# The first block of a fused convolution and MLP kernel: other load order, first weight unit rounded in thirds, copies on another queue, output weights combined later

## Chip, cores and metric

One core of one Trainium2 chip runs the whole kernel. The metric is device time in microseconds (us), the median of several executions. A profiled span is about 1.7 us shorter than the time the same execution reports (2428.01 beside 2429.71 for the kernel before), so spans are compared with spans and times with times.

## The reference

A causal depthwise convolution with 7 taps, softmaxed per head, then `silu(x @ w_in) @ w_out`, over 32768 tokens of 192 channels with 2048 hidden columns:

```python
w = np.exp(weight - weight.max(-1, keepdims=True))        # (8 heads, 7 taps)
w = w / (w.sum(-1, keepdims=True) + 1e-9)
x_pad = zeros(pad) ++ x                                   # pad = 6 positions in front of each sequence
out = einsum('hk,bskhg->bshg', w, windows(x_pad))         # (8, 4096, 192) -> 32768 x 192
h = out @ w_in                                            # w_in arrives as float64
g = h * (1 / (1 + exp(-h)))
return (g @ w_out).astype(float32)
```

(Shortened; `zeros`, `++` and `windows` stand for the padding and indexing code.)

## The kernel before

The tokens go through in 32 blocks of 1024. Blocks 2 to 32 use a recombined product scheme, laid out in a plan of slots. The first block is plain: while it is transposed, convolved and multiplied, the weights are loaded in four units of `w_in` and four of `w_out`. They are 64-bit words, which VectorE takes apart and rounds to float32 with integer operations (`rounded`). `ws` is a copy of a rounded unit `wr` with the two partition halves swapped. GpSimd combines some of the weights for the later scheme. The parts that matter here:

```python
def load(b):                                   # x of a block: 12 DMAs, three channel thirds k of four
    nat = nats[b] = xpool.tile(...)
    for k in range(NK):
        for i in range(P // SQ):
            (nc.sync if b or k or i % 2 else nc.scalar).dma_start(out=nat[...], in_=x_v[...])

# ... wexp (taps) on nc.scalar, six values of x on nc.gpsimd ...
load(0)

def rounded(dst, key, shared):                 # whole unit: 768 columns per instruction
    # eight VectorE operations + two on ScalarE (shared) or two more on VectorE
    # ...

def round_in(j):
    rounded(wr[j].rearrange("p a k c -> p (a k c)"), ("i", j), j < 2)
    for e in range(2):
        nc.scalar.dma_start(out=ws[j][R * e : R * e + R], in_=wr[j][R - R * e : 2 * R - R * e])

load_in(0, nc.scalar)
load_in(1, nc.sync)
# ... softmax of the taps: max, subtract, Exp on ScalarE, sum, reciprocal, ...

for k in range(NK):                            # first block
    turn_in(0, k)                              # transpose
    for i in range(K):
        conv(0, k, i)                          # seven taps on VectorE
    spread(0, k)                               # four DMAs nat -> dup
    if k == 0:
        round_in(0)
        load_in(2, nc.sync)
round_in(1)
load_in(3, nc.sync)
for j in range(NJ):
    up_plain(0, j)                             # 64x512 matmuls into 8 PSUM banks, Silu on ScalarE
    # ... round_in(j + 2) or round_out, load_out, load(1) ...
# ... conv of block 2, combine_in, plain down-projection ...
for j in range(NJ):
    combine_out(j)
```

`raw`, the tile that a unit is loaded into, comes from a pool of three buffers (`tag="t"`) that also serves `two`, the scratch of the rounding. `nat` and `dup` have one buffer each.

## Time and profile before

| | kernel before |
|---|---|
| time, median | 2429.41 us (3 runs, 2428.07 to 2429.82) |
| profiled span | 2428.0 us |
| TensorE busy | 98% |
| VectorE busy from first transpose to the second unit | 9.77 to 39.85 us without a gap |
| TensorE ends k=2 of the first up-projection | 40.46 us |
| TensorE runs without a gap from | 43.12 us |
| block 2, first product | 117.81 us |
| TensorE's end, to the end of the span | 2417.55, 10.47 us |

To read it: from 43.12 us on TensorE is the chain until close to the end, so the total is a start, a body of fixed length and a tail. The prediction shows the lines that carry this.

The executions of the kernel before in all the rounds below fall into two groups, at 2427.9 to 2428.4 and at 2429.1 to 2430.9. The profile above is of the longer group (2429.71).

### The profile page before, as it was taken

How to read it: one execution, taken by the hardware profiler on the slowest of the kernel's cores; microseconds unless marked ns; L12 is line 12 of the kernel's file. 1: busy time of each engine (PE TensorE's matmuls, PEld its weight loads, DVE VectorE, ACT ScalarE, POOL GpSimd, SP SyncE). 2: the span in 40 equal slices, each digit the busy share in tenths (PEclk: the TensorE clock that was granted, in tenths of full speed). 3: DMA queues.
4: the chain of work that ended last, by engine and by line, in shares of the span. 5: the costliest groups of instructions: out<-in, count | busy, mean ns of one | idle time of the engine just before them, and what ended most of it. 6: DMA issues, size and time to landing. Idle time of an engine off the chain costs nothing.

```text
span 2428.0 us, 42997 instructions
## 1 busy us (share of the span) xinstructions
PE 2391.3 (98%) x17744; PEld 939.2 (39%) x17744; DVE 2075.0 (85%) x2810; ACT 980.8 (40%) x1840; POOL 62.0 (3%) x92
## 2 busy tenths in 40 slices
PE   5999999999999999999999999999999999999998
PEld 3334433344333344333443333443334433334432
DVE  8898888898888988888988889888889888898875
ACT  2145433345333454333453334543334533345432
POOL 2300000000000000000000000000000000000000
PEclk9999999999999999999999999999999999999999
DMA  7321222212222222222122222122221222222210
GB/s 153 75 44 35 36 53 53 40 38 38 45 53 43 42 39 36 53 53 40 38 38 44 53 44 46 35 36 53 53 40 38 37 45 53 43 43 39 36 40 14
DMA packets 452260, 111.64 MB, mean 46 GB/s; under 512 B 421792, under 2 KB 426912, under 8 KB 452064
## 3 DMA queue, kind: packets, MB, share of 16 engines
q1 hardware_dynamic: 447056, 105.84, 22.6%
q10 hardware_dynamic: 4784, 2.78, 0.6%
q8 instruction: 139, 2.28, 0.4%
q14 instruction: 57, 0.47, 0.1%
q0 software_dynamic: 224, 0.27, 0.0%
HBM read 31.49 MB, written 25.17 MB: 23 GB/s over the span
## 4 chain that ended last, share of the span: by engine, by line
PE 98%; DVE 1%; DMA 1%; ACT 0%; issue 0%; ACTq 0%; POOL 0%; SPq 0%; POOLq 0%; DVEq 0%
PE ps L411 48%; PE ps L468 46%; PE ps L519 2%; PE ps L375 1%; DMA nat<-in_x_dram 0%; DVE nat L325 0%; DVE two L111 0%; DMA raw<-in_moe_w_in_dram 0%; DVE cmb L570 0%; DVE mh L111 0%; DVE xt L305 0%; POOL out_dram L587 0%; SPq L165 0%; ACT L385 0%; DVE osb L580 0%
## 5 line engine op out<-in xcount | busy, mean ns | idle before, releaser
L411 PE MATMUL ps<-dup,ws 64*128 64x512 f32 x2480 | 869.9, 589 | 0.0
L468 PE MATMUL ps<-g,wo 128*32 128x512 f32 x2976 | 662.0, 593 | 0.0
L435 DVE TENSOR_TENSOR g<-u,ps 128x512 f32<-128x512 f32 x744 | 485.8, 680 | 119.1 <-PE ps L411 89.8
L411 PE MATMUL ps<-win,wr 64*128 64x512 f32 x1488 | 567.7, 589 | 0.0
L468 PE MATMUL ps<-t,wo 128*32 128x512 f32 (+1 forms) x4464 | 500.7, 450 | 0.0
L432 ACT ACTIVATE g<-g 128x512 f32<-128x512 f32 x744 | 444.7, 631 | 97.4 <-DVE g L435 97.4
L411 PEld LDWEIGHTS ps<-dup,ws 64*128 64x128 f32 x2480 | 363.0, 187 | 292.0 <-issue 277.9
L468 PE MATMUL ps<-t,wx 128*32 128x512 f32 x2976 | 453.1, 592 | 0.0
L325 DVE SCALAR_TENSOR_TENSOR nat<-xt,taps,nat 128x512 f32<-128x512 f32 x576 | 432.2, 750 | 15.1
L411 PE MATMUL ps<-dup,wr 64*128 64x512 f32 x992 | 419.9, 596 | 0.0
L426 ACT COPY u<-ps 128x512 f32<-128x512 f32 x496 | 277.7, 588 | 229.1 <-PE ps L411 226.1
L558 ACT COPY cmb<-ps 96x512 f32<-96x512 f32 x31 | 18.0, 581 | 832.1 <-PE ps L468 832.1
L452 DVE TENSOR_TENSOR t<-g 128x1024 f32<-128x1024 f32 x248 | 299.8, 1220 | 27.0 <-PE ps L468 27.0
L452 DVE TENSOR_TENSOR t<-g,t 128x1024 f32<-128x1024 f32 x248 | 303.4, 1224 | 17.9 <-PE ps L468 7.4
L411 PEld LDWEIGHTS ps<-win,wr 64*128 64x128 f32 x1488 | 233.4, 187 | 175.5 <-issue 147.2
L468 PEld LDWEIGHTS ps<-t,wo 128*32 128x32 f32 x4464 | 178.3, 110 | 222.6 <-issue 204.9
L411 PE MATMUL ps<-win,ws 64*128 64x512 f32 x496 | 242.2, 589 | 0.0
L468 PE MATMUL ps<-g,wx 128*32 128x512 f32 x1488 | 234.7, 592 | 0.0
L468 PEld LDWEIGHTS ps<-t,wx 128*32 128x32 f32 x2976 | 121.9, 110 | 278.2 <-issue 268.7
L570 DVE TENSOR_TENSOR cmb<-cmb,ps 96x512 f32<-96x512 f32 x155 | 105.7, 682 | 141.9 <-ACT u L555 139.7
L411 PEld LDWEIGHTS ps<-dup,wr 64*128 64x128 f32 x992 | 160.5, 187 | 128.2 <-issue 114.3
L468 PEld LDWEIGHTS ps<-g,wo 128*32 128x32 f32 x2976 | 168.5, 110 | 97.7 <-issue 97.7
(53 smaller groups left out, 1191.3 us busy)
## 6 DMA issues: line engine op xcount, KB each, us to landing
dup<-nat SPq DMA_DIRECT2D x384, 128.0 KB, 2.3
nat<-in_x_dram SPq DMA_DIRECT2D x382, 64.0 KB, 2.4
out_dram<-osb SPq DMA_DIRECT2D x376, 64.0 KB, 1.9
raw<-in_moe_w_out_dram SPq DMA_DIRECT2D x8, 384.0 KB, 3.5
raw<-in_moe_w_in_dram SPq DMA_DIRECT2D x12, 192.0 KB, 4.2
ws<-wr ACTq DMA_DIRECT2D x8, 192.0 KB, 5.6
raw<-in_moe_w_in_dram ACTq DMA_DIRECT2D x4, 192.0 KB, 5.9
xt<-xt SPq DMA_DIRECT2D x31, 4.5 KB, 1.9
```

The costliest lines, as they stand in the source:

```text
L325: nc.vector.scalar_tensor_tensor(out=dst, in0=src, scalar=tap, in1=dst, op0=ALU.mult, op1=ALU.add)
L375: nc.tensor.matmul(hs[a, n, e], rows(wr[j], e)[:, a, k, :], rows(d, e)[:, n, k, :], start=k == 0, stop=k == NK - 1,)
L411: nc.tensor.matmul(bk[b, m, bn], rows(w, half), rows(v, half), start=first, stop=True, skip_group_check=True,)
L426: pin(copy(u, bk[b, m, "1"]))
L432: pin(nc.scalar.activation(g, g, AF.Silu))
L435: pin(nc.vector.tensor_tensor(g, us.pop((b, m, i)), bk[b, m, bn], op=ALU.add))
L452: pin(nc.vector.tensor_tensor(t[i // 2][:, i % 2, :], u, v, op=ALU.subtract))
L468: nc.tensor.matmul(accs[b][i][SQ * q : SQ * q + SQ, cols], lhs[:, e, SQ * c : SQ * c + SQ], rhs[:, e, cols] if i < 5 else rhs[:, e, ts(q, ...
L519: nc.tensor.matmul(acc[k][R * n : R * n + R, :], wo[j][:, a, e, R * k : R * k + R], gs[b, j, a][:, n, e, :], start=j == 0 and a == 0 and e ...
L558: pin(nc.scalar.copy(c[0], acc[0][0:n, :]))
L570: pin(nc.vector.tensor_tensor(out_, u, v, op=ALU.add))
```

## The change

The intent is to have TensorE's long run begin sooner. The Exp table is loaded by a dummy before it is wanted, and four slow DMA issues leave ScalarE. The first unit of `w_in` is rounded a third at a time so that each third of channels can be multiplied as soon as it is convolved. The copies `ws` leave ScalarE's queue. The combination of `w_out` moves into the second block.

```diff
-    def load(b):
+    def load(b, ks=range(NK)):
...
-    load(0)
+    load(0, (0,))
+
+    warm = const.tile([P, 1], F32, name="warm")
+    vec.memset(warm, 0.0)
+    nc.scalar.activation(warm, warm, AF.Exp)
...
-    def round_in(j):
-        rounded(wr[j].rearrange("p a k c -> p (a k c)"), ("i", j), j < 2)
-
-        for e in range(2):
-            nc.scalar.dma_start(
+    def round_in(j, k=None):
+        ...
+        else:
+            rounded(wr[j][:, :, k, :], words[:, :, k], j < 2)
+        if k in (None, NK - 1):
+            del raws["i", j]
+            for e in range(2):
+                nc.gpsimd.dma_start(
                     out=ws[j][R * e : R * e + R], in_=wr[j][R - R * e : 2 * R - R * e]
                 )
...
-    load_in(0, nc.scalar)
+    load_in(0, nc.sync)
+    load(0, (1, 2))
     load_in(1, nc.sync)
...
         spread(0, k)
-        if k == 0:
-            round_in(0)
-            load_in(2, nc.sync)
+        round_in(0, k)
+    load_in(2, nc.sync)
     round_in(1)
...
-    for j in range(NJ):
-        combine_out(j)
...
-        run(b, plan[:NU])
+        run(b, plan[: NU // 4])
+        if b == 1:
+            for j in range(NJ):
+                combine_out(j)
+        run(b, plan[NU // 4 : NU])
```

More of the change, by code (lines that the diff above doesn't have):

```diff
@@ L118 @@
     nats, xts, gs = {}, {}, {}
-    def load(b):
-        nat = nats[b] = xpool.tile([P, NK, TB // SQ, SQ], F32, tag="nat", name="nat")
-        for k in range(NK):
+    def load(b, ks=range(NK)):
+        if b not in nats:
+            nats[b] = xpool.tile([P, NK, TB // SQ, SQ], F32, tag="nat", name="nat")
+        nat = nats[b]
+        for k in ks:
             for i in range(P // SQ):
@@ L172, in load_out, with rounded, like @@
             queue.dma_start(out=raw[:, a, :, :], in_=out32[a, q])
-    def rounded(dst, key, shared):
-        words = raws.pop(key).rearrange("p (n t) -> p n t", t=2)
-        lo, hi = words[:, :, 0], words[:, :, 1]
+    def rounded(dst, words, shared):
+        lo, hi = words[:, :, :, 0], words[:, :, :, 1]
+        x_, y_ = dst.shape[1:]
+        def like(t):
+            return t.rearrange("p (x y) -> p x y", x=x_)
+        n = x_ * y_
         two = tpool.tile([P, 4 * TB], I32, tag="t", name="two")
-        ex, st = two[:, 0:WC], two[:, WC : 2 * WC]
-        mh = xpool.tile([P, 4 * TB], I32, tag="cmb", name="mh")[:, 0:WC]
+        ex, st = like(two[:, 0:n]), like(two[:, n : 2 * n])
+        mh = like(xpool.tile([P, 4 * TB], I32, tag="cmb", name="mh")[:, 0:n])
         one = 1 << 20
@@ L213, in rounded @@
         )
-    def round_in(j):
-        rounded(wr[j].rearrange("p a k c -> p (a k c)"), ("i", j), j < 2)
-        for e in range(2):
-            nc.scalar.dma_start(
-                out=ws[j][R * e : R * e + R], in_=wr[j][R - R * e : 2 * R - R * e]
-            )
-    def round_out(q):
-        rounded(wo[q].rearrange("p a e d -> p (a e d)"), ("o", q), False)
+    def round_in(j, k=None):
+        words = raws["i", j].rearrange("p (a k c t) -> p a k c t", a=2, k=NK, t=2)
+        if k is None:
+            rounded(
+                wr[j].rearrange("p a k c -> p a (k c)"),
+                words.rearrange("p a k c t -> p a (k c) t"),
+                j < 2,
+            )
+        else:
[4 more added lines that the diff above has]
+                nc.gpsimd.dma_start(
+                    out=ws[j][R * e : R * e + R], in_=wr[j][R - R * e : 2 * R - R * e]
+                )
+    def round_out(q):
+        rounded(
+            wo[q].rearrange("p a e d -> p a (e d)"),
+            raws.pop(("o", q)).rearrange("p (a x t) -> p a x t", a=2, t=2),
+            False,
+        )
     def comb(out, u, v, op):
```

## The prediction

> **What bounds the kernel now.** I read the page first, then the chain of waits in order of time, then the timeline of the first 125 us engine by engine. Page, part 1 (engine, busy us, share, instructions):
>
> ```profile
> PE 2391.3 (98%) x17744; PEld 939.2 (39%) x17744; DVE 2075.0 (85%) x2810; ACT 980.8 (40%) x1840; POOL 62.0 (3%) x92
> ```
>
> TensorE (PE) is busy 98% of the 2428.0 us span. The chain (start, us, what) shows where it isn't:
>
> ```profile
> 39.88 0.47 ACTq L219
> 40.35 0.04 issue
> 40.39 0.75 ACTq L219
> 41.14 0.03 issue
> 41.17 1.28 ACT L385
> 42.45 0.01 issue
> 42.47 0.60 ACT g L385
> 43.07 0.04 issue
> 43.12 33.35 PE ps L375 x143
> 76.46 41.35 PE ps L519 x192
> 117.81 37.97 PE ps L411 x176
> 155.78 36.22 PE ps L468 x384
> ```
>
> From 43.12 on the chain is TensorE alone up to 2413.72; then 14.3 us of tail that the diff doesn't touch. So the time is (moment from which TensorE runs without a gap) + about 2370 + tail, and a change confined to the first block can move only that moment, and the clock TensorE has just after it. Blocks 2 to 32 repeat every 74.2 us (117.81, 192.00, ...) whatever the start was.
>
> What sets 43.12 is a serial line through VectorE (DVE) and then ScalarE (ACT). From the timeline (start, us, engine, line, op, count, idle before):
>
> ```profile
> 6.33 1.28 ACT L280 ACT_TABLE_LOAD   x1 [6.33 <-DMA nat<-in_x_dram]
> 8.60 0.22 DVE L111 TENSOR_TENSOR wexp<-wexp,wred 128x56 f32<-128x56 f32 x1
> 9.77 0.70 DVE L305 STREAM_TRANSPOSE xt<-nat 128x512 f32<-128x512 f32 x1
> 33.37 1.02 DVE L111 TENSOR_SCALAR two<-raw 128x768 int32<-128x768 int32 x2
> 35.81 4.65 PE L375 MATMUL ps<-dup,wr 64*128 64x512 f32 x16 [0.33 <-DMA dup<-nat]
> 38.89 0.96 DVE L111 SCALAR_TENSOR_TENSOR wr<-mh,two 128x768 f32<-128x768 f32 x1
> ```
>
> VectorE has no gap over 0.1 us from 9.77 to 39.85: third k=0 (transpose and 7 taps, to 15.6), the whole first w_in unit (15.64 to 21.39), k=1 (21.30), k=2 (27.17), the second unit (33.37 to 39.85). ScalarE then still has to issue two copies of ws (in its queue behind that unit), load the table for Silu and evict one bank: 3.26 us. TensorE was through at 40.46, and waits 2.66 us with full PSUM banks. That wait has a second price, in the windows view (window, length, busy us of PE, PEld, DVE, ACT, POOL, granted clock, DMA share, GB/s):
>
> ```profile
> 36.90:40.20 3.30, 3.30 (x15) 1.80 (x12) 3.20 (x5) 0.00 (x0) 0.00 (x0) 1.00 0.06 13
> 40.30:43.60 3.30, 0.64 (x2) 0.29 (x2) 3.30 (x7) 2.42 (x4) 0.00 (x0) 1.00 0.96 225
> 43.70:47.00 3.30, 3.30 (x9) 1.72 (x9) 2.77 (x3) 2.79 (x6) 0.77 (x2) 0.50 1.04 182
> 47.10:50.50 3.40, 3.40 (x19) 1.94 (x17) 3.38 (x6) 1.08 (x2) 1.72 (x3) 1.00 1.06 318
> ```
>
> For 3.4 us after the idle window the granted clock is 0.50: nine matmuls begin where about sixteen do at full clock (pairs start every 0.85 us, then every 0.43), a loss of about 1.8 us.
>
> **What the Trainium skill says.** "ScalarE: Activation LUTs", section What ACT_TABLE_LOAD costs, gives about 1283 ns for a load; both loads here took 1.28 us. "TensorE: Matmul & The Clock Gate", Part 1, gives half clock after an idle window of about 3.4 us and full clock after a busy one; the table above agrees, though the idle window was not empty (about 0.7 us of work). "DMA: Bandwidth & Descriptors", section Issuing engines are not separate DMA queues, says that another issuing engine saves only sequencer time. Before, that time is visible: four w_in issues hold ScalarE from 2.39 to 6.31. "GPSIMD Engine Reference", section Key points, has GpSimd share SBUF interfaces with VectorE. Seen here: a tap costs 0.75 us, but 0.82 while GpSimd (POOL) combines weights from 27.8, and the second unit takes 6.48 us, the first 5.75.
>
> **The change part by part.**
>
> 1. Start. The w_in issues leave ScalarE, and a dummy Exp (ready after a small memset) loads the Exp table at about 2.4 to 3.7. wexp lands at 4.33 as before, so the real Exp can run at 4.85 instead of 7.63: 2.78 us. The taps would be ready at 7.1, the transpose could follow, but it also needs the four loads of x for k=0. From the records of landings these came at 4.66, 5.37, 5.81 and 7.44. Now w_in stands right behind two of them in the sync queue, so I take 7.7 (estimate). VectorE starts 2.07 us earlier.
>
> 2. Rounding by thirds. Instructions of 768 columns become three of 256. One-input ones take 0.555 us at 768, two-input ones 0.955; the 56-column ones (0.22 in the line above) show 0.15 fixed. So at 256: 0.15 + 0.405/3 = 0.285, and 0.15 + 0.805/3 = 0.42. ScalarE's two go from 0.84 to about 0.41. Laid out with their dependences (successors that don't depend overlap by 0.09), a third takes 2.57 us where the whole took 5.66: 3 x 2.57 = 7.7, so 2.05 us more. This eats the gain of 1. Its benefit, k=0's weights at about 16 instead of 21.4, is TensorE work that isn't the last thing waited for.
>
> 3. GpSimd contention. The copies of ws now wait on GpSimd's own queue for all of unit 0, so the first combine moves from 27.8 to about 38. The taps of k=2 return to 0.75 (0.3 us), the second unit to about 5.75 plus 0.2 for a copy and descriptor writing (0.5 us).
>
> VectorE: 7.7 + 3 x (5.87 + 2.57) + 5.95 = 38.97, against 39.85: 0.9 us earlier.
>
> 4. ScalarE. The ws issues are gone. Its two operations for the second unit end at about 35.9, the Silu table is in by 37.2, and it evicts as TensorE finishes. The first bank frees at about 38, before the second unit's weights. So the 3.26 us tail behind VectorE disappears; the second unit's last write is the release.
>
> 5. TensorE on k=2 needs the last third's weights (about 33.2) and its dups (last landing 37.57 before, now about 34.7). After a gap of about 5 us it probably begins at half clock; eight pairs end between 37.6 and 39.3 depending on when full clock returns. So the gapless run begins at 39.0, on average 39.1: 4.0 us earlier. The gap before it is at most 1.4 us, so no window should be nearly idle: the loss of 1.8 us goes, with a chance I put at 0.85: 1.5 us.
>
> 6. w_out combined later. On GpSimd the four last combines already stood behind the wait for the end of the plain down-projection (112.76); the built order is nearly the same, and their first user runs at 155.78. Worth 0.
>
> Sum: 4.0 + 1.5 = 5.5 us off 2429.4, or 2424.
>
> **The rivals.** (a) *Later weights become the new wait.* The third unit's load starts only after the whole of unit 0 is rounded (about 33 instead of 20.42) and may land at 39 to 41; VectorE may idle up to 2 us and have it rounded by 45.5 to 47.6. TensorE wants it at 39.1 + 10.3 = 49.4. The fourth unit: ready about 54.5, wanted at 59.7. w_out 1: ready 62.6, wanted 70. I don't expect a stall; if one came, it would give back 1 to 3 us: 2425 to 2427. (b) *Block 2 arrives before its inputs.* It would start at about 112.3, and its win and dup tiles were ready at 111.63 and 111.26, set by VectorE's rounding, not by TensorE. The margin was 6 us and falls to under 2 (the k=2 dup is used 2 us in, the last win later still). If VectorE slips by 3 us, the gain is capped near 3: 2426. (c) *The small instructions cost more than I reckon, or x for k=0 lands late behind w_in.* Each microsecond goes straight into 39: with both bad by 1 us, 2426. (d) *The clock stays at half* for one more window: 2425.7. (e) *All is hidden anyway*: against it stands that the 2.66 us wait is on the chain and nothing behind it has a gap.
>
> **Range and chances.** All parts act in 45 us of 2429; even the whole lead-in gone would be 1.8%. A change over 2% either way would need a break in the 74.2 us period of the later blocks, whose instructions the change leaves alone: 0.005 each. Best case (taps bound at 7.1, k=2 quickly at full clock, no contention) about 7.5 us, and 2429.82 to 2428.07 is the spread of before; so the low end is 2421.5. Two rivals at once leave 2 us: 2427.2 as the high end.
>
> **What would show it right or wrong.** In the changed profile: first table load at about 2.4; first transpose at 7.1 to 8.2; rounding thirds of about 2.6 us; last write of the second unit near 39.0; no ScalarE piece between that write and the gapless run of TensorE; granted clock 1.00 right after; the second block's products starting near 112.3 and every block 74.2 us after that. Wrong would be: a chain that goes back through a load of w_in or a ws copy after 40; a half clock window in the long run of up-projections; a wait of the second block's first products on dup or win; a gapless start later than 41.

## The result, and the profile after

The changed kernel took 2425.83 us (median of 6 runs, 2425.70 to 2426.55), the kernel before in the same rounds 2429.50 (6 runs). The ratio is 0.9986, 95% interval 0.9973 to 0.9999. A ratio is the mean time of one kernel's fast runs over that of the other's of the same rounds, so it is not quite the ratio of the medians. The gain is 3.7 us where 5.5 was predicted. It is within the range and within 2%.

The page of the kernel after, part 1 (engine, busy us, share, instructions):

```profile
PE 2389.0 (99%) x17744; PEld 944.2 (39%) x17744; DVE 2076.5 (86%) x2827; ACT 981.7 (40%) x1845; POOL 66.4 (3%) x100
```

The chain of waits after (start us, us, what):

```profile
38.06 0.14 issue
38.20 31.17 PE ps L403 x144
69.37 41.35 PE ps L547 x192
110.72 20.47 PE ps L439 x88
131.19 0.10 issue
131.30 19.15 PE ps L439 x88
150.45 36.22 PE ps L496 x384
```

Set these beside the chain before. The long run starts at 38.20 in place of 43.12 (4.92 us sooner), and no piece of ScalarE stands in front of it now. The up-projections take 31.17 in place of 33.35 (2.18 less). The plain down-projection is the same 41.35. So block 2 starts 7.09 us sooner, more than the whole predicted gain. Then its products take 20.47 + 0.10 + 19.15 = 39.72 us in place of 37.97: 1.75 us are given back in one block. Every later block keeps a lead of 5.33 us. The windows view after (same columns as in the prediction, the window that was nearly empty before) shows the larger part of why the up-projections shrank:

```profile
40.30:43.60 3.30, 3.30 (x18) 1.73 (x16) 2.98 (x5) 1.09 (x2) 3.01 (x6) 1.00 1.23 201
```

TensorE is now busy in it throughout, and the clock stays at 1.00 from 36.55 us to the tail. The half-clock window is not gone: it lies at 33.14 to 36.55, before the second unit's last write, where it costs the long run nothing. The clock is not all of the 2.18 us. The matmuls start two at a time, one step of 0.43 us after another. The first six steps of the long run took 4.37 us before and 2.65 after: 1.72 us are the clock. The other 0.46 are one step more: before, the two of a pair had come apart by a step (a single matmul at 43.12 and another at 75.88), so the run had 73 starts where the changed kernel has 72.

Where did 1.75 us in block 2 come from? First the timeline of VectorE after (start, us, engine, line, op, tiles, and in brackets the idle time before with what ended it):

```profile
40.62 1.33 DVE L111 TENSOR_SCALAR two<-raw 128x768 int32<-128x768 int32 x2 [2.57 <-DMA raw<-in_moe_w_in_dram]
```

VectorE finishes the second unit at 38.05 and then waits 2.57 us for the load of the third, which is now issued only when the last third of unit 0 has been rounded. TensorE does not notice at the time. But VectorE has about 70 us of rounding and convolving to do before block 2, and it carries the delay there: the convolution of block 2 ended at 107.16 us before and ends at 108.52 after, although TensorE arrives 7 us sooner. The view of waits from 104 to 152 us (who waits for what, us in total, times, longest) has these lines after, and no line of either kind before:

```profile
DVE xt L333 <- DMA nat<-in_x_dram: 1.6, 2, 1.3
PEld ps L439 <- DMA dup<-nat: 1.3, 2, 0.8
```

TensorE's weight loads wait for the last `dup` copies of block 2, which land at 112.80 and 113.10 (110.69 and 111.26 before) when the products have begun at 110.72. VectorE later waits for the next `nat`, whose load is issued late because the single buffer came free late.

The last piece of the account is the tail, which the prediction said the diff doesn't touch. From TensorE's end to the end of the span it is 11.86 us where it was 10.47. The DMA views of the last stores, 7 us from about 3.5 us after TensorE's end (queue that issues, DMAs, KB each, median us from issue to landing), before:

```profile
out_dram<-osb ACTq DMA_DIRECT2D x3, 64.0 KB, 3.2
out_dram<-osb POOLq DMA_DIRECT2D x3, 64.0 KB, 3.5
```

And after:

```profile
out_dram<-osb ACTq DMA_DIRECT2D x3, 64.0 KB, 4.0
out_dram<-osb POOLq DMA_DIRECT2D x3, 64.0 KB, 4.1
```

The stores are issued at the same moments after TensorE's end in both (the last at 5.41 and 5.42 us), but the last one lands after 4.61 us in place of 3.53. The account of the spans: 4.92 + 2.18 - 1.75 - 1.39 = 3.96, against 2428.0 - 2424.1 = 3.9.

### The profile page after: what moved, and what is told of

Read it like the earlier page. It is cut to its first block, busy times and chain, and to the rows that moved or that the text cites. A ratio compares the mean times of both kernels' runs of the same rounds, so it can differ in the third digit from the quotient of the medians.

```text
span 2424.1 us, 43022 instructions
## 1 busy us (share of the span) xinstructions
PE 2389.0 (99%) x17744; PEld 944.2 (39%) x17744; DVE 2076.5 (86%) x2827; ACT 981.7 (40%) x1845; POOL 66.4 (3%) x100
## 4 chain that ended last, share of the span: by engine, by line
PE 98%; DVE 1%; DMA 0%; SPq 0%; ACT 0%; issue 0%; POOL 0%; ACTq 0%; POOLq 0%; DVEq 0%
PE ps L439 49%; PE ps L496 46%; PE ps L547 2%; PE ps L403 1%; DVE nat L353 0%; DVE two L111 0%; SPq L127 0%; DMA nat<-in_x_dram 0%; DVE cmb L598 0%; DMA raw<-in_moe_w_in_dram 0%; DVE mh L111 0%; DVE wr L111 0%; DVE xt L333 0%; POOL out_dram L615 0%; DVE osb L608 0%
```

## The experiments

Twelve kernels ran, all with correct results, in four batches. Within a batch they shared the chip and the runs of the kernel before (median 2429.1, 2429.17, 2429.63 and 2429.41 us, 9 runs each). Key times from the traces, in us; "landing" is the last store's landing after TensorE's end:

| kernel | time, median | long run starts | block 2 starts | its products | landing | tail |
|---|---|---|---|---|---|---|
| before | 2429.1 to 2429.6 | 43.12 | 117.81 | 37.97 | 8.94 | 10.47 |
| after | 2425.83 | 38.20 | 110.72 | 39.72 | 10.03 | 11.86 |
| e1, unit 2 loaded early | 2423.89 | 39.29 | 111.86 | 37.97 | 9.94 | 11.77 |
| e2, ws copies on ScalarE again | 2432.60 | 39.14 | 119.59 | 37.97 | 9.96 | 11.72 |
| e3, unit 0 whole | 2423.36 | 38.39 | 111.23 | 37.97 | 9.97 | 11.77 |
| e4, early combine_out | 2425.99 | 38.27 | 110.79 | 39.93 | 9.98 | 11.80 |
| e5, start alone | 2427.01 | 40.30 | 113.77 | 37.97 | 9.97 | 11.78 |
| e6, ws on GpSimd alone | 2424.41 | 39.75 | 112.34 | 37.97 | 8.95 | 10.50 |
| e7, e3 with repeats | 2423.46 | 36.81 | 109.65 | 38.55 | 9.98 | 11.77 |
| e8, e3, unit 3 from GpSimd | 2423.30 | 37.34 | 110.19 | 37.97 | 9.96 | 11.68 |
| e9, e3, unit 2 from ScalarE | 2422.96 | 39.07 | 111.91 | 37.97 | 9.97 | 11.40 |
| e10, e7, unit 2 from ScalarE | 2423.44 | 36.99 | 109.83 | 38.35 | 9.98 | 11.42 |
| e11, e6, half of unit 0 from sync | 2423.55 | 38.80 | 111.42 | 37.97 | 8.95 | 10.99 |
| e12, e7, wider dummy tile | 2423.58 | 37.01 | 109.85 | 38.58 | 9.93 | 11.73 |

**Theory A:** the late load of unit 2 makes VectorE idle, and that comes out as TensorE's stall in block 2. Its rival: the stall comes from something else in block 2, such as the combination of `w_out` that the change put there.

### e1: unit 2 loaded early, into a buffer of its own

```diff
+        if key == ("i", 2):
+            raws[key] = xpool.tile([P, 2 * WC], I32, tag="raw2", name="raw")
...
         round_in(0, k)
-    load_in(2, nc.sync)
+        if k == 0:
+            load_in(2, nc.sync)
```

> The changed kernel, but the third unit of w_in gets a buffer of its own (6 KB a partition) and is loaded right after the first dups instead of after all three thirds are rounded. Theory A (the second block's products lose 1.75 us, 39.72 against 37.97, because VectorE idles 2.57 us at 38.05 for this load and reaches the second block's inputs that much later): the idle of 2.57 us is gone, the dups of k=2 of the second block land about 2 us earlier (112.8 and 113.1 before), the second block's products take 38.0 to 38.4 us, the gapless start stays near 38.2, and the time falls by 1.4 to 1.8 us, to about 2424.2. Rival B (the loss comes from GpSimd's combining of w_out beside VectorE's win, 2.77 us for one instruction): the idle goes, but the second block still takes about 39.5 us and the time stays at 2425.8.

Measured: 2423.89 us (2423.75 to 2425.08), ratio to before 0.9979 [0.9966, 0.9993], 1.94 us less than the changed kernel. VectorE's idle time before unit 2 is gone, and in the chain of e1 the products of block 2 are one unbroken piece again:

```profile
111.86 37.97 PE ps L442 x176
```

That is 37.97 where the changed kernel has 39.72: theory A holds. This profile even fell in an execution with two half-clock windows in a row (31.93 to 38.76), so it reaches block 2 1.1 us later than the changed kernel and still ends TensorE 0.6 us sooner. A first try, with a fourth buffer in the shared pool, did not fit into SBUF and was not run.

### e2: the copies of ws on ScalarE's queue again

```diff
-                nc.gpsimd.dma_start(
+                nc.scalar.dma_start(
                     out=ws[j]...
```

> The changed kernel, but the copies wr to ws are issued by ScalarE again, as before the change. Theory A (most of the gain is the ScalarE piece behind VectorE's last write of the second unit, plus the half-clock window it causes): the last write stays near 38.1, then 1.25 us of issue, 1.28 of table load and 0.6 of eviction, gapless start near 41.2 (3.0 us later), probably a half-clock window after it (1.8 us), and no loss in the second block (1.75 us back): 2427 to 2429. Rival C (the copies' place doesn't matter, it is the earlier start that gives the gain): stays within 0.7 of 2425.8. Side question, the tail: from TensorE's end to the end of the span it was 14.28 us before and 15.71 after the change; if the copies on GpSimd's queue cause this, it is back at 14.3 here, else it stays at 15.7.

Measured: 2432.60 us (2431.84 to 2432.75), ratio 1.0014 [1.0001, 1.0027]: slower than the changed kernel by 6.8 us, and slower than before. The direction was expected, the place was not. The long run did start early (39.14), but the chain of e2 is broken at 55 us:

```profile
55.35 0.47 ACTq L242
...
56.51 0.61 ACT g L413
...
57.16 21.08 PE ps L403 x84
```

In this chain ScalarE does its work in the order of the program. The issue of a copy that waits for unit 3 (written at 55.31) stands in front of the evictions, and TensorE, now ahead of VectorE, has filled its banks and waits from 53.77 to 57.16. After that wait the clock is at half from 55.5 to 62.3. So the move of the copies is what makes the changed kernel's earlier start usable. (In e5 below, without the thirds, the copies are on ScalarE too, and the long run still starts 2.82 us sooner than before.) The tail stayed at 11.72, so the copies on GpSimd's queue are not what lengthened it.

### e3: unit 0 rounded whole again

```diff
-        round_in(0, k)
-    load_in(2, nc.sync)
+        if k == 0:
+            round_in(0)
+            load_in(2, nc.sync)
```

> The changed kernel, but the first unit of w_in is rounded whole after the first third of x, as before the change, and unit 2 is loaded right after that. Theory A (the thirds cost VectorE 2.05 us and give nothing that the end waits for, and they delay unit 2's load): the last write of the second unit comes 1.5 to 2.1 us earlier, near 36.3, gapless start near 36.4, no idle for unit 2, second block's products 38.0 to 38.4 us: 2421.8 to 2422.6, faster than both kernels. Rival D (the thirds are a source of the gain, since TensorE has all of k=0 and k=1 done earlier and k=2 starts in time): gapless start at 39 or later and 2426 or more.

Measured: 2423.36 us (2423.14 to 2424.44), ratio 0.9978 [0.9965, 0.9991]: 2.5 us faster than the changed kernel, but not quite what was expected. The second unit is written at 37.08 (38.05 after), unit 2 is not waited for beyond 0.7 us, and block 2 has its 37.97. The chain of e3 shows what bounds the start in place of the second unit:

```profile
30.57 2.25 DMA dup<-nat
32.82 0.04 issue
32.86 37.02 PE ps L403 x160
```

The chain goes back through the `dup` copies of k=2, not through the second unit: TensorE begins k=2 at 32.86, at half clock from 33.68 to 37.09, and is through at 38.90. So rounding by thirds cost 0.97 us at the second unit, and the late load of unit 2 that came with it cost the 1.75 us in block 2 (e1 keeps the thirds, loads early and doesn't lose them). It bought nothing that the traces show: its benefit, earlier products, is work that isn't waited for. The start itself is no earlier in e3 (38.39 beside 38.20).

### e4: w_out combined in the first block again

```diff
-        run(b, plan[: NU // 4])
-        if b == 1:
-            for j in range(NJ):
-                combine_out(j)
-        run(b, plan[NU // 4 : NU])
+        run(b, plan[:NU])
```

(with `combine_out` back in its old place.)

> The changed kernel, but w_out is combined right after the first block again, as before the change. The built order differs only in where GpSimd's third combine of the fourth unit and the combines of w_out stand. Theory A (this part is worth nothing): within 0.4 us of 2425.8, second block's products still 39.5 to 39.9 us. Rival B (it matters for the second block): differs by more than 1 us either way.

Measured: 2425.99 us (2425.88 to 2426.11), ratio 0.9987 [0.9974, 1.0001]: 0.2 us from the changed kernel, and block 2 still takes 39.93. Theory A's rival falls, and the later combination is worth nothing.

### e5 and e6: one part alone

e5 is the kernel before with only the dummy Exp and the new order of loads:

```diff
-    load(0)
+    load(0, (0,))
+    warm = const.tile([P, 1], F32, name="warm")
+    vec.memset(warm, 0.0)
+    nc.scalar.activation(warm, warm, AF.Exp)
...
-    load_in(0, nc.scalar)
+    load_in(0, nc.sync)
+    load(0, (1, 2))
```

> The kernel before with only the first part of the change: dummy Exp and the new order of loads (first unit of w_in on the sync queue, rounded whole after k=0; copies of ws still on ScalarE; w_out combined early). Theory A (the parts add up as the sum has them): first transpose at about 6.9, 2.9 us earlier than before; last write of unit 1 at about 36.9; ScalarE's 3.26 us behind it stays, so the long run of TensorE starts at 40.0 to 40.4, 2.7 to 3.1 us earlier than before; the half-clock window after a nearly idle one may stay. Rival B (the two parts only work together: the ws copies on ScalarE's queue block it more when it starts earlier, as in the second experiment): start later than 41. On the tail, theory T (the longer landing of the last stores comes with the moved loads): tail 11.6 to 11.9 and a time of 2427 to 2428.5; rival U (it comes from another part): tail 10.4 to 10.6 and 2426 to 2427.

e6 is the kernel before with one word changed:

```diff
-            nc.scalar.dma_start(
+            nc.gpsimd.dma_start(
                 out=ws[j]...
```

> The kernel before with only the copies of ws moved from ScalarE's queue to GpSimd's. Theory A: unit 1 is still written at about 39.4 to 39.9, ScalarE has evicted by then, TensorE ends k=2 at 40.0 to 40.5 and goes straight on: the long run starts at 39.9 to 40.5 where it was 43.12, no half-clock window after it, so 2.7 to 3.2 us plus 1.8 us of clock less up to 1 us lost in the second block: 2424.5 to 2426. Rival B (the queue of ScalarE was not what held the start; the Silu table and the eviction alone take as long): start at 41.5 or later, 2427 or more. On the tail, theory T: 10.4 to 10.6 as before, since the loads are where they were; rival U: 11.6 to 11.9, and the time 1.3 us longer than the first figure says.

Measured: e5 2427.01 us (2426.74 to 2429.69), ratio 0.9993 [0.9980, 1.0005]; e6 2424.41 us (2424.28 to 2424.57), ratio 0.9980 [0.9967, 0.9994]. The one word alone is worth 4.8 us, more than the whole change. The interval of e5 includes 1, so its gain is read from the trace, not from the times; and it doesn't part the dummy Exp from the new order of loads. The chain of e5:

```profile
38.35 1.28 ACT L392
...
40.30 32.12 PE ps L382 x142
```

The second unit is ready at 37.04, 2.8 us sooner than before, and then the same 3.26 us pass in ScalarE: two issues (37.07 to 38.32), the Silu table shown above, one eviction. The chain of e6 has none of it:

```profile
33.10 2.41 DMA dup<-nat
35.50 0.04 issue
35.55 35.44 PE ps L375 x160
```

TensorE starts k=2 at 35.55 and has no gap after that. The granted clock is 1.00 from 25.5 us on. Ends of TensorE beside before's: e5 4.04 us sooner, e6 5.47, and both and more together, the changed kernel, 5.33. The tail tells the parts apart as well: 11.78 in e5, 10.50 in e6. So the longer tail comes with the start part.

### e7: repeated matmuls to keep TensorE busy

e3, with ten matmul calls put in front (the eight of k=0 and the first two of them once more; the trace shows two records for each). The real k=0 then starts the sums afresh, so the result is the same:

```diff
+        if not j:
+            order = order[:4] + order[:1] + order
...
-                    stop=k == NK - 1,
+                    stop=k == NK - 1 or len(order) > 12 and at < 5,
```

> The third experiment (first unit rounded whole) plus ten repeated matmuls: the k=0 products of the first up-projection are computed one and a quarter times over, with the same result, so that TensorE stays busy from 19 us until k=1 and k=2 come. Theory C (in the third experiment the long run was bound by half clock from 33.7 to 37.1 after a window half idle): k=0 ends at about 29, k=1 at about 32.5, k=2 runs at full clock from 32.9 to 36.3, and the next unit starts when unit 1 is written, at 37.1 to 37.3 in place of 38.4: about 1.1 us less than the third experiment, 2422.2. Rival D (the clock follows something other than TensorE's idle time, or the repeats push k=2 back): start at 38.4 or later, 2423.3 or more.

Measured: 2423.46 us (2423.15 to 2423.74), ratio 0.9976 [0.9964, 0.9989]: no less than e3. By its mechanism theory C is right. In the chain of e7 TensorE runs without a gap from its first matmul, at full clock from 24.64:

```profile
18.78 49.51 PE ps L405 x211
...
109.65 19.29 PE ps L441 x88
```

The next unit starts at 36.81. But block 2 is then reached at 109.65, 1.6 us sooner than in e3, before VectorE has its inputs, and its products take 38.55: 0.58 lost. The rest is in how the runs of e3 group: 2423.14, 2423.18 and 2423.36, and then 2424.43 and 2424.44. The profiled run of e3, with its half-clock window, is of the longer group (2424.43), so the median of e3 hardly pays for that window. e8 and e9 are alike: e9's profile shows a half-clock window and took 2424.76; e8's shows none and took 2423.30. The runs of e6 and e7 lie within 0.3 and 0.6 us.

### e8 to e12: the tail

**e8** is e3 with `load_in(3, nc.gpsimd)` in place of `nc.sync`, to test whether the number of packets that the sync queue has carried matters:

> The third experiment with the load of unit 3 of w_in moved from the sync queue to GpSimd's, so that the sync queue carries as many packets as in the kernel before. Theory T2 (the tail depends on how far the sync queue's ring of descriptors has advanced): tail back to 10.4 to 10.6 and 1.2 us less than the third experiment, about 2422.1. Rival U2 (it depends on something else): tail 11.6 to 11.9 and 2423.2 to 2423.6, as long as unit 3 is still rounded before it is wanted at about 57.

Measured: 2423.30 us (2422.92 to 2424.76), ratio 0.9977; tail 11.68 with the same 447056 packets on the sync queue as before. That theory falls.

**e9** is e3, and **e10** is e7, with `load_in(2, nc.scalar)` in place of `nc.sync`. **e11** is e6 with two of the four loads of unit 0 on the sync queue. They ask the same of ScalarE's queue:

> The third experiment (first unit rounded whole) with the load of unit 2 of w_in issued by ScalarE, which is idle then, so that ScalarE's hardware queue carries 4144 packets, as many as in the kernel before with only the ws copies moved; the sync queue carries as many as before. Theory V (the longer landing of the last stores goes with a smaller number of packets that ScalarE's queue has carried: the two kernels with 4144 and 4784 have a tail of 10.5, all with 3312 or 3952 have 11.7 to 11.9): tail 10.4 to 10.6, and 1.2 us less than the third experiment, about 2422.0 to 2422.2. Rival W (it goes with the dummy Exp or with the order in which the loads are issued at the start): tail 11.6 to 11.9 and 2423.0 to 2423.5.

> The seventh experiment (repeated matmuls in the idle stretches of the first up-projection) with the load of unit 2 of w_in issued by ScalarE. Theory V: tail 10.4 to 10.6, about 2422.2, and no run in the group that is about 1.2 us longer, as in the seventh. Rival W: tail 11.6 to 11.9, about 2423.4.

> The kernel before with the ws copies on GpSimd's queue (the sixth experiment) and two of the four loads of unit 0 of w_in moved from ScalarE's queue to the sync queue: ScalarE's queue then carries 3728 packets in place of 4144; no dummy Exp. Theory V: tail 11.6 to 11.9, so 1.2 us lost there against what the start gains (0 to 1.5 us, since ScalarE gets to its Exp some 2 us sooner): 2424.2 to 2425.6. Rival W: tail 10.4 to 10.6, 2423 to 2424.4.

Measured: e9 2422.96 us (2422.83 to 2424.78), ratio 0.9975; e10 2423.44 us (2422.89 to 2423.72), ratio 0.9974; e11 2423.55 us (2423.52 to 2423.85), ratio 0.9975. The last store lands 9.97 and 9.98 us after TensorE's end in e9 and e10, late as in the changed kernel, and 8.95 in e11, early as before. Theory V falls on both sides. The tail of e11 as a whole, 10.99, fits neither expectation, because 0.5 us more pass in it after that landing; the landing is the cleaner measure.

What separates the two sorts is then the dummy Exp or the order of the first loads. The built programs suggest a third thing: the tile of the dummy, one column wide, takes 32 bytes of SBUF in each partition and moves every tile allocated after it. The tile that the output is stored from (`osb`) stands at address 113152 in before, e6 and e11, and at 113184 in the changed kernel (127520 in e1, also 32 past a multiple of 64). **e12** is e7 with the tile 64 bytes wide:

```diff
-    warm = const.tile([P, 1], F32, name="warm")
+    warm = const.tile([P, 16], F32, name="warm")
```

> The seventh experiment with one edit: the tile of the dummy Exp is 16 columns wide (64 bytes in each partition) in place of one. The built programs show that the one-column tile takes 32 bytes of SBUF and moves every later tile by 32: the tile that the output is stored from stands at address 113152 (a multiple of 64) in the kernels without the dummy Exp and at 113184 in those with it; here it stands at 113216, again a multiple of 64. Theory X (the stores' short reads from SBUF take longer from an address that is not a multiple of 64): the packets of the sync queue return to a 90th percentile of 13 ns (16 in all kernels with the one-column tile), the tail to 10.4 to 10.6, and the time is 1.2 us less than the seventh experiment, about 2422.2. Rival Y (the dummy Exp itself, or the order of the first loads, makes the last stores land later): 16 ns, a tail of 11.6 to 11.9 and about 2423.4.

Measured: 2423.58 us (2423.18 to 2423.69), ratio 0.9976; landing 9.93, tail 11.73. As stated, theory X falls: a multiple of 64 does not help. What remains is the alignment to more than that. "DMA: Bandwidth & Descriptors" of the Trainium skill, section How a descriptor splits into AXI transactions, says that a transaction must start from a 256-byte-aligned address. A store reads `osb` in pieces of 128 bytes. At 113152 = 442 x 256 no piece crosses a multiple of 256; at 113184, 32 past one, every second piece does (160 to 288), and at 113216 too (192 to 320). The traces fit this in part. The 128-byte packets of the two hardware queues in the tail took 11.9 ns on average in before, e6 and e11, and 14.6 to 14.7 in the changed kernel, e1, e5 and e7, and 15.05 in e12. The tail is not special in this: where stores in the body of the kernel run beside no other transfer, the packet records of the same traces give 11.69 ns in before, e6 and e11, 12.76 to 12.77 in the changed kernel, e1, e5 and e7, and 13.13 in e12, the same early and late. e7 and e12 differ by the width of the dummy's tile alone, and with it the addresses, so these most likely act on the stores; but as many pieces cross in e7 as in e12, so crossing is not the whole of it.

The loads of x into `nat`, which the move shifts too, took 12.75 ns in isolation in all of these. They don't tell before from the changed kernel, since every second piece crosses in both (`nat` at 69952 and 69984, 64 and 96 past a multiple of 256). In e12 (70016, 128 past) none crosses, and they were no faster. So all this is a fit over kernels, and not a test: none ran with the dummy Exp and `osb` at a multiple of 256. The cause of the longer tail stays open between the address and the dummy Exp or the load order themselves.

No kernel was faster than e9 by its median. e3, e7, e8, e9, e10, e11 and e12 lie within 0.7 us of one another, 5.7 to 6.7 us under before, so they are one result. e11 is among them with no dummy Exp at all.

## Why the prediction was right, and where it was not

**What bounds the kernel** was right. The changed kernel's chain is again a start, a body of the same length per block, and a tail.

**Point 1, start:** right, and small in size. The table loads at 2.39 to 3.67 us, and the taps are ready at 6.94, as reckoned. The transpose came at 6.86, not 7.7: the guess that x would land late behind the first unit was wrong by 0.84 us. This is almost the whole difference between the long run's predicted start (39.0) and 38.20.

**Point 2, thirds:** right. From one transpose to the next it takes 15.29 to 23.74 = 8.45 us, against 5.87 + 2.57 = 8.44. **Point 3, contention:** right. The six taps of k=2 took 4.69 us in all, as those of k=0 did, and the second unit took 5.76 (32.29 to 38.05). In e3, where GpSimd combines earlier, six taps of k=2 took 5.02 and the unit 6.62 (30.46 to 37.08).

**Point 4, ScalarE:** right. The Silu table was in at 36.23, and the evictions follow it. e5 and e6 show that this is the part that pays.

**Point 5, TensorE on k=2:** right in mechanism. It began at 32.31, ran at half clock from 33.14 to 36.55, and ended at 38.02. The clock term was put at 1.8 x 0.85 = 1.5; 1.72 of the 2.18 by which the up-projections shrank are the clock. The other 0.46, the pair that had come apart, the prediction didn't see. Such a half-clock window isn't in every execution, so the worth of this term in a median is less sure than one profile says.

**Point 6, w_out combined later:** worth 0, as said; e4 shows it.

**The sum** of 5.5 left out two terms, and these are where it failed. (i) Rival (a) named the idle time of VectorE for the third unit ("up to 2 us"; 2.57 measured) and then judged it by TensorE's need of that unit, in the same block. There it was indeed harmless. Rival (b) named the damage, block 2 arriving before its inputs, but took it for a cap that a slip of 3 us would reach. The two were one mechanism: the idle time of (a) is the slip that (b) needed. It cost 1.75 us with a slip of 1.36 us at the end of block 2's convolution, since the start was sooner than predicted as well. e1 takes the idle time away and gets 1.94 us back. (ii) "14.3 us of tail that the diff doesn't touch" was wrong: counted the same way, it is 15.7 us. e5 and e6 place this in the start part; which piece of it is open, as told under e12. That the total still came within 2 us of the forecast is in part luck: the two terms left out (3.14 us) were half offset by the two that came out larger (1.60).

With 0.92 more at the start, 0.68 more in the up-projections (0.22 of it the clock, 0.46 the step), 1.75 and 1.39 less, the sum is 5.5 + 0.92 + 0.68 - 1.75 - 1.39 = 3.96, the difference of the spans.

## What to carry to other kernels

Judge an engine's idle time off the critical path by the next deadline that its work has, not by the first user of the tile it waited for: the delay stays with the engine until something waits for it. Try the parts of a change singly, since here one word moved to another queue was worth more than the whole, and a part that only brings work forward that nobody waits for (the thirds) cost what another had gained. A new small tile in front of the others moves every address behind it (whether that lengthened the tail here stays open), so look at the landing of the stores before calling a tail untouched.

## What the Trainium skill lacked or had wrong

- "TensorE: Matmul & The Clock Gate", Part 1, gives half clock after an idle window of about 3.4 us, and says that the effect varies with the phase of the window. The runs fit this (those of e3 and of e9 fall into two groups, 1.1 to 1.9 us apart), but the window need not be idle. The page's section "A second HAM failure mode: psum-queue depth-cycling" (HAM is its word for the monitor that sets this clock) has a kernel whose short pauses were enough, without figures for them. In e3 the clock fell at 33.68 after a window of 3.41 us in which TensorE worked about 2.0 us (to 31.45, and again from 32.86, a gap of 1.4), and in e9 at 35.03 after about 2.0. In e6 (gap 34.07 to 35.55) and e8 (31.56 to 33.13) the clock did not fall with windows of about 1.9 and 2.05 us of work. What share of a window counts is on no page, and work in it alone doesn't decide it.
- "DMA: Bandwidth & Descriptors", section How a descriptor splits into AXI transactions, has the 256-byte boundary and counts what crossing it costs in transfer beats, but gives no time for it. If that is the cause here, it is 14.6 ns in place of 11.9 for a 128-byte store packet, and 1.1 us on the landing of the last stores.
- The same page, section Issuing engines are not separate DMA queues, calls the sequencer time saved by another issuing engine usually small. It doesn't say that an issue which waits for its data holds up all that stands behind it on its engine; the TensorE page calls ScalarE's queue strictly first in, first out, but names neither DMA issues nor a cost. Here this was the larger part: e6 gained 4.8 us and e2 lost 6.8 us by that queue alone.
